# Batch 0 of an FFT and mixture-of-experts kernel: its first stage handed to the second by twelve transfers inside SBUF

## The chip, the cores and the metric

The kernel runs on one core of a Trainium2 chip. The metric is the device time of one execution in microseconds (us). Before the change the median of 8 runs is 1258.31 us, the lowest 1257.81, the highest 1259.43.

## The reference

The input `x` has shape (8, 2496, 256): 8 batches of 2496 tokens with 256 channels, float32. The reference does two things in a row:

```
X = fft(fft(x, axis=1), axis=2).real        # over the sequence, then over the channels
t = X.reshape(19968, 256)
logits = t @ w_gate                          # 8 experts
e = argmax(logits); gate = softmax(logits)[e]
out = gate * (relu(t @ w1[e]) @ w2[e])       # w1[e]: 256 x 1024, w2[e]: 1024 x 256
```

Each token goes to one expert alone, so the kernel sorts the transformed tokens by expert and multiplies them in blocks.

## The kernel before

**Stages.** The transform over 2496 = 104 x 24 positions is done in two stages of matrix products. The *first stage* of a batch (`first`, lines 325 to 347) takes `x` in three thirds, one tile `xq` each ([112, 8, 256], 896 KB). VectorE (DVE) adds each row to its mirror and folds the channels (`fold`, `fold_d`); TensorE (PE) multiplies with the waves `con["w1"]`, two steps to a half (`half1`), twelve steps in all; ScalarE (ACT) copies a half from PSUM to `t1`, and when a third is whole, a transfer writes it to the DRAM tensor `Td[b]` (448 KB; on ACT's queue for batches 0 and 1, on SyncE's (SP) queue later). `first` is a generator of twelve steps. `regroup` (line 351) reads `Td[b]` back in another order into two tiles `t4`, which have the 120 rows of five groups on the partitions; a batch has NG = 11 such groups.

The *second stage* (`second`, line 361) turns the column H of `t4` (`pr`), multiplies each group with `m2` into `zz`, and multiplies stretches of 128 of `zz` with `rd` (`p3`), which gives half the channels and the router's logits at once; two DVE operations build the rows of 128 tokens and their mirrors (line 410), ACT writes the mirrored channels. After five stretches `route` (line 416) finds expert and place of 1280 rows, in three steps and a last part, and puts ten transfers into `waiting`. Such a transfer (`send`, line 462) is an indirect scatter of 128 rows on GpSimd's (POOL) queue into `Xs`, where the tokens stand by expert. A batch takes 20 of them. The second stage is a generator of 19 steps.

The *experts* (`experts`, line 730) take blocks of `Xs`: rows and weights are fetched on SP, rows transposed by DVE (`turn`), multiplied (`ph`, `py`), scaled by ACT and scattered to the output by POOL.

**Order.** The order is written out by hand: each engine and each queue runs its instructions in the order in which the program issues them. For batch 0 everything before the experts is at the end of the program: the loads of `x`, waves and tables; `first(0)` whole; the loads of batch 1; the two `regroup` of batch 0; then the products of `rt` with the router's weights (`pg`); then seven steps of batch 1's `first` (`early`); then `second(0)`, in which every other step is followed by one more step of `early`, and each step by one `send`. `early` ends with the two `regroup` of batch 1.

Then the main loop asks `experts` for work. Each `yield 0, False` of it runs one step of the side list and one `send`. The side list weaves the plan of the first blocks (`close(0)`) with batch 1's second stage and batch 2's first stage (`mixed(1)`). Once the plan's table is there, all rows of batch 0 are sent, the first blocks are fetched, nine more `yield 0, False` follow (line 784), and then comes the first turn, the transpose of the first block, and the first `ph`. Of the eighteen side steps up to there the last nine hold the rest of the plan and batch 1's second stage up to its fourth stretch.

**Counters.** The framework gives a transfer issued from SP or ACT one of eight completion counters in turn; the issuing engine waits where the counter's last transfer is still under way.

Of the kernel before, what the change touches and what calls it, by code (L numbers as in the profile page):

```python
# [12 lines left out]
F32 = mybir.dt.float32  # L13
BF16 = mybir.dt.bfloat16
I32 = mybir.dt.int32
ALU = mybir.AluOpType
# [16 lines left out]
HALF = -(-NG // 2)  # L33
LAST = NW * 128 - (NG - 1) * GP
NT = B * S
E, F = 8, 1024
FC = F // 128
# [9 lines left out]
def free(ap, offset, *dims):  # L47
    return bass.AP(ap.tensor, ap.offset + offset, [list(ap.ap[0])] + [list(d) for d in dims])
# [167 lines left out]
def kernel(ctx: ExitStack, tc, x, w_gate, w1, w2, out):  # L216
    nc = tc.nc
    vec, act, pool = nc.vector, nc.scalar, nc.gpsimd

    def mm(o, lhsT, rhs, start=True, stop=True, **kw):  # L220
        nc.tensor.matmul(o, lhsT=lhsT, rhs=rhs, start=start, stop=stop, **kw)  # L221
# [4 lines left out]
    def const_dram(name, v):  # L226
        return nc.inline_tensor(v, name=f"c_{name}").ap()
# [36 lines left out]
    consts = shape_consts()  # L264
# [4 lines left out]
    con, k = {}, 0  # L269
# [12 lines left out]
    waves = const_dram("w1", consts["w1"])  # L282

    def load(b, q):

        if b < B:
            xq = xp.tile([NP, 8, D], F32, tag="xq", name="xq", bufs=3)
            row = (b * NQ + q) * NA
            nc.sync.dma_start(out=xq[:].rearrange("p j d -> p (j d)"), in_=x[row:row + NP])
            ahead[b, q] = xq[0:NA]  # L290

    def fold_d(o, a, n):
# [29 lines left out]

    ahead = {}

    def first(b):
# [23 lines left out]
    base = con["cap"]  # L349

    def regroup(b, h):
        t4 = sp.tile([128, HALF, D], F32, tag="t4", name="t4")
        n = min(HALF, NG - h * HALF)
        nc.sync.dma_start(
            out=t4[:, 0:n], in_=bass.AP(Td[b].tensor, Td[b].offset + h * HALF * GP * D,
                                        [[D, 128], [GP * D, n], [1, D]]))
        ahead[b, "t4", h] = t4

    zz = cp.tile([128, 2, NW * 128], F32, name="zz")

    def second(b):
# [368 lines left out]
    def experts(todo):  # L730
# [44 lines left out]
        for k, (b, size, last, at) in enumerate(todo):  # L775
            n, m = size // 128, BIG // size
            if not k:
                while todo[0][:3] not in tabs:
                    yield 0, False
                fetch_some(0, 1)  # L780
                while b not in whole:
                    yield 0, True
                fetch_some(0)
                for _ in range(9):
                    yield 0, False
                for xT in turn(b, size, xbs[0][0]):
                    pass
# [20 lines left out]
            if both:  # L808
# [4 lines left out]
                parts = [slice(lo, lo + fp) for lo in range(0, FC // 2, fp)]  # L813
# [133 lines left out]
        yield from through(b)  # L947

    vec.memset(ones[:], 1.0)
    act.dma_start(out=con["w1"][:, 0:4], in_=waves[:, 0:4])  # L950
    load(0, 0)
    load(0, 1)
    nc.sync.dma_start(out=con["w1"][:, 4:], in_=waves[:, 4:])
    load(0, 2)
    nc.sync.dma_start(out=table[:], in_=const_dram("table", packed))
    nc.sync.dma_start(out=con["rt"][:], in_=const_dram("rt", consts["rt"]))
    nc.sync.dma_start(out=wg[:], in_=w_gate)
# [6 lines left out]

    tabs, whole = {}, set()
    todo = in_order()
    for _ in first(0):
        pass
    load(1, 0)
    load(1, 1)  # L970
    regroup(0, 0)
    regroup(0, 1)
    load(1, 2)
    nc.sync.dma_start(out=bt[:], in_=const_dram("blocks", cv))
    sent(unordered(nc.sync.dma_start(
        out=Xs[E * CAP:].rearrange("(k p) w -> p k w", k=BLK // 128), in_=bc(pad[:], 1, BLK // 128)), "xs"), 0)
# [104 lines left out]
```

## Time and profile before

| | us |
|---|---|
| median of 8 runs | 1258.31 |
| the profiled execution: its time | 1257.62 |
| the profiled execution: its span, first to last instruction | 1255.8 |
| PE busy | 1207.7 (96%) |
| DVE busy | 759.6 (60%) |
| POOL busy | 447.5 (36%) |
| ACT busy | 431.3 (34%) |
| batch 0: last third of x landed, first use by DVE | 17.74 |
| batch 0: third write to Td issued, on ACT | 25.75 |
| batch 0: two reads into t4 issued, on SP | 28.88 and 29.33 |
| batch 0: first product of the second stage (pr) | 33.75 |
| batch 0: first scatter on POOL | 53.13 |
| batch 1: reads into t4 issued; first product of its second stage | 55.02; 60.37 |
| batch 0: fetch of the first block issued | 82.84 |
| first turn: transpose on DVE, first expert product on PE | 86.56, 87.33 |

All times are from one profiled execution, counted from its first instruction. The profile has a busy time per engine, the same in 40 slices of the span, the clock that PE was granted, the queues of the DMA engines (q1 is SP's, q10 is ACT's, q0 is POOL's), a timeline, the waits with what ended them, and the chain of waits that ends with the last instruction. L221 is the line of the helper that issues every matmul, so PE's instructions are told apart by their tiles: `s` is the first stage, `pr`, `p` and `rk` are the second stage and routing, `ph` and `py` the experts.

### The profile page before, as it was taken

To read this page: it belongs to the slowest core of one execution; us is meant where nothing else is said; L and a number is where in the kernel's file an instruction comes from. 1 tells how busy PE (TensorE), PEld (TensorE's weight loads), DVE (VectorE), ACT (ScalarE), POOL (GpSimd) and SP (SyncE) were. 2 spreads that over 40 slices of the span, in tenths; PEclk is the share of its full clock that TensorE was granted. 3 is DMA by queue.
4 is the path that set the end of the run, shared out by engine and by line. 5 is a ranking of instruction groups with operands and counts; after the bars stand their busy time and mean duration, and the time that the engine had idled before them with its cause. 6 is when DMAs were issued, how large, how long until landed. Compare 5 with 4: busy or idle time off the path is not lost.

```text
span 1255.8 us, 22295 instructions
## 1 busy us (share of the span) xinstructions
PE 1207.7 (96%) x7289; PEld 1076.2 (86%) x7289; DVE 759.6 (60%) x1804; ACT 431.3 (34%) x1167; POOL 447.5 (36%) x527
## 2 busy tenths in 40 slices
PE   5749999999999999999999999999999999999997
PEld 4648988777788899888988899889999999999996
DVE  4446434343456688566865578686888784444653
ACT  1424333333243433434343333432333332222222
POOL 0245427054117421471226613472364241111112
PEclk6869999999999999999999999999999999999999
DMA  8859898873548434673336435453346328888887
GB/s 242 280 177 337 305 313 310 222 242 117 151 154 263 147 117 156 189 232 113 102 128 208 137 98 166 135 177 101 107 138 187 113 106 285 276 286 284 280 290 284
DMA packets 163216, 249.79 MB, mean 199 GB/s; under 512 B 118601, under 2 KB 130227, under 8 KB 143516
## 3 DMA queue, kind: packets, MB, share of 16 engines
q1 hardware_dynamic: 146327, 203.28, 50.8%
q0 software_dynamic: 15888, 42.14, 9.1%
q10 hardware_dynamic: 885, 2.94, 0.7%
q8 instruction: 59, 0.97, 0.3%
q14 instruction: 57, 0.47, 0.1%
HBM read 194.91 MB, written 54.83 MB: 199 GB/s over the span
## 4 chain that ended last, share of the span: by engine, by line
PE 82%; DVE 9%; DMA 3%; ACT 2%; issue 2%; POOL 0%; SPq 0%; POOLq 0%; DVEq 0%; ACTq 0%
PE py L221 25%; PE ph L221 13%; PE a L221 11%; PE c L221 9%; PE p L221 6%; PE b L221 6%; PE d L221 5%; PE e L221 4%; PE s L221 3%; DMA xq<-in_x_dram 1%; DVE xT L584 1%; DMA Td<-t 1%; DVE y L684 1%; DMA Xs<-rows,pi 1%; DVE hT L636 1%
## 5 line engine op out<-in xcount | busy, mean ns | idle before, releaser
L236 POOL DMA_INDIRECT out_dram<-y,ro x163 | 161.5, 991 | 625.2 <-ACT y L680 301.2
L221 PE MATMUL py<-w_sb,hT 128*128 128x256 f32 x1504 | 339.5, 379 | 0.0
L221 PEld LDWEIGHTS py<-w_sb,hT 128*128 128x128 f32 x1504 | 281.4, 190 | 36.9 <-issue 1.0
L236 POOL DMA_INDIRECT Xs<-rows,pi x160 | 162.5, 1016 | 109.9 <-DVE rows L410 54.6
L221 PE MATMUL ph<-xT,w_sb 128*128 128x128 f32 (+2 forms) x992 | 171.6, 329 | 11.1 <-DVE xT L584 11.0
L221 PEld LDWEIGHTS ph<-xT,w_sb 128*128 128x128 f32 x992 | 136.7, 193 | 35.1 <-issue 16.8
L410 DVE SCALAR_TENSOR_TENSOR rows<-p,zs 128x129 f32<-128x129 f32 x160 | 48.9, 348 | 129.8 <-ACT lg L408 125.8
L221 PE MATMUL a<-xT,w_sb 128*128 128x256 f32 (+1 forms) x512 | 117.8, 357 | 0.0
L838 DVE TENSOR_SCALAR hT<-ph 128x512 f32<-128x512 f32 x43 | 29.7, 691 | 123.7 <-PE ph L221 64.0
L587 ACT ACTIVATE xT<-xT 128x256 f32<-128x256 f32 (+1 forms) x94 | 36.5, 388 | 179.0 <-DVE xT L584 140.6
L892 ACT ACTIVATE y<-py,xb 128x256 f32<-128x256 f32 x94 | 44.6, 475 | 152.3 <-PE py L221 152.1
L221 PEld LDWEIGHTS a<-xT,w_sb 128*128 128x128 f32 x512 | 88.6, 190 | 9.7
L636 DVE TENSOR_TENSOR hT<-hT,b 128x512 f32<-128x512 f32 x57 | 39.2, 687 | 75.8 <-PE b L221 50.2
L646 ACT ACTIVATE hT<-a 128x512 f32<-128x512 f32 x57 | 34.0, 597 | 134.1 <-PE a L221 131.1
L221 PE MATMUL s<-xq,w 104*112 104x256 f32 (+2 forms) x208 | 61.4, 418 | 15.2 <-DVE xq L297 11.1
L469 POOL CAST pi<-due 128x1 int32<-128x1 f32 x140 | 44.9, 320 | 66.7 <-ACT due L468 66.6
L221 PE MATMUL a<-w_sb,hT 128*128 128x128 f32 x528 | 66.0, 276 | 0.0
L221 PEld LDWEIGHTS a<-w_sb,hT 128*128 128x128 f32 x528 | 63.1, 192 | 0.7
L221 PEld LDWEIGHTS p<-table,t 120*128 120x128 f32 x352 | 53.4, 201 | 11.0 <-ACT t L372 2.8
L221 PE MATMUL c<-xT,ws 128*128 128x256 f32 (+1 forms) x256 | 60.3, 362 | 1.0 <-DVE hT L642 0.2
L584 DVE STREAM_TRANSPOSE xT<-xb 128x512 f32<-128x512 f32 (+1 forms) x91 | 56.2, 631 | 7.5 <-DMA xb<-Xs 7.5
L221 PE MATMUL p<-table,t 120*128 120x120 f32 (+1 forms) x352 | 56.6, 285 | 3.0 <-ACT t L372 2.0
(149 smaller groups left out, 2054.5 us busy)
## 6 DMA issues: line engine op xcount, KB each, us to landing
w_sb<-in_moe_w_dram SPq DMA_DIRECT2D x132, 1024.0 KB, 6.8
xq<-in_x_dram SPq DMA_DIRECT2D x24, 896.0 KB, 8.7
xb<-Xs SPq DMA_DIRECT2D x112, 128.0 KB, 3.4
Td<-t SPq DMA_DIRECT2D x18, 448.0 KB, 5.4
t<-Td SPq DMA_DIRECT2D x8, 768.0 KB, 6.9
t<-Td SPq DMA_DIRECT2D x8, 640.0 KB
xb<-Xs SPq DMA_DIRECT2D x52, 64.0 KB, 4.4
xb<-Xs SPq DMA_DIRECT2D x88, 32.0 KB, 4.4
```

Source lines behind the costliest of these rows:

```text
L221: nc.tensor.matmul(o, lhsT=lhsT, rhs=rhs, start=start, stop=stop, **kw)
L236: return unordered(pool.indirect_dma_start(out=dst, out_offset=bass.IndirectOffsetOnAxis(ap=idx, axis=0), in_=rows, in_offset=None, bounds ...
L410: vec.scalar_tensor_tensor(rows[:, k + m, 0:NY], p3[:, 0:NY], zs[:, 0:1], zs[:, 1:], op0=ALU.add, op1=op)
L469: pool.tensor_copy(idx, due[:])
L584: vec.transpose(free(xT[:], 256 * h, [32, n // 32], [BIG, 2], [1, 32]), free(xb, 512 * h, [64, n // 32], [1, 2], [2, 32]))
L587: act.activation(odd, odd, ACTF.Copy, scale=-1.0)
L636: vec.tensor_tensor(h12, h11, b[:], op=add)
L646: act.activation(h11, a[:], ACTF.Relu)
L684: vec.tensor_tensor(o, o, p[:], op=add)
L838: vec.tensor_scalar(o, ph[:], 0.0, None, op0=ALU.max)
L892: act.activation(y[:, i % 2], py[:], ACTF.Copy, scale=meta[:, i, 1:2])
```

## The change

In batch 0 the first stage no longer goes through `Td[0]`. The waves are loaded in another order of columns (`wp`, 110 columns of NG by ten), so that the product of step s has on its partitions, for each of ten (group row, part) pairs, the eleven groups. A new function `first_whole` does batch 0's first stage: it adds, folds and multiplies by halves of a third; after each half ACT copies it to `t1` (the last half in two copies), and each step is sent by a transfer of its own from `t1` to every twelfth partition of `t4s`, 110 KB in rows of 1 KB. Eleven of the twelve go on ACT's queue, that of step 11 on SP's. `t4s` is one tile for both halves of all groups; the `regroup` of later batches writes into it. Three ACT copies (`natural`) bring the waves back to the old order in `con["w1"]` for the later batches, whose unused columns DVE sets to zero.

The last third of `x` is loaded in two pieces, and the waves in three, with the pieces in between. `load(1, q)` is issued right after third q of batch 0. Three steps of batch 1's `first` stand before `second(0)` instead of seven, and twelve `yield 0, False` before the first turn instead of nine.

```
+    wp = bp.tile([128, NS + 3, NR], F32, tag="w2", name="wp", bufs=3)[0:NA]
+    order = consts["w1"][:, :, 0:NR].reshape(NA, NS + 3, NG, 2 * NU).swapaxes(2, 3)
+    waves = const_dram("w1", order.reshape(NA, NS + 3, NR))
...
+    def first_whole():
+        pm0 = xp.tile([NA, D], F32, tag="pm0", name="pm0")
+        for q in range(NQ):
+            xq = ahead.pop((0, q))
+            t1 = xp.tile([NP, 4, D], F32, tag="t1", name="t1")
+            for lo in (0, 2):
+                end = q == NQ - 1 and lo
+                a, m = xq[:, lo:lo + 2], xq[:, 4 + lo:6 + lo]
+                n = 2
+                if end:
+                    n = 1
+                    fold_d(pm0[:], m[:, 1], 1)
+                vec.tensor_tensor(a[:, 0:n], a[:, 0:n], m[:, 0:n], op=ALU.add)
+                fold_d(m, a, 2)
+                ps = pm_.tile([NP, 2, D], F32, tag="m", name="s1")
+                for i in range(2):
+                    s = 4 * q + lo + i
...
+                        mm(o, columns(s), m[:, i])
...
+                if end:
+                    for i in range(2):
+                        act.copy(t1[0:NR, lo + i], ps[0:NR, i])
+                else:
+                    act.copy(t1[0:NR, lo:lo + 2], ps[0:NR])
+                for i in range(2):
+                    s = 4 * q + lo + i
+                    (nc.sync if s == NS - 1 else act).dma_start(out=t4s[s:GP:NS, 0:NG], in_=t1[0:NR, lo + i])
+            load(1, q)
+        for lo in range(0, NS + 3, 5):
+            natural(lo, lo + 5)
+        for h in range(2):
+            ahead[0, "t4", h] = t4s[:, h * HALF:(h + 1) * HALF]
...
+    def natural(lo, hi):
+        n = hi - lo
+        act.copy(free(con["w1"][:, lo:hi], 0, [NP, n], [2 * NU, NG], [1, 2 * NU]),
+                 free(wp[:, lo:hi], 0, [NR, n], [1, NG], [NG, 2 * NU]))
...
     def regroup(b, h):
-        t4 = sp.tile([128, HALF, D], F32, tag="t4", name="t4")
+        t4 = t4s[:, h * HALF:(h + 1) * HALF]
...
+    t4s = cp.tile([128, 2 * HALF, D], F32, name="t4s")
...
-                for _ in range(9):
+                for _ in range(12):
                     yield 0, False
...
-    act.dma_start(out=con["w1"][:, 0:4], in_=waves[:, 0:4])
+    vec.memset(con["w1"][:, :, NR:], 0.0)
+    act.dma_start(out=wp[:, 0:4], in_=waves[:, 0:4])
     load(0, 0)
     load(0, 1)
-    nc.sync.dma_start(out=con["w1"][:, 4:], in_=waves[:, 4:])
-    load(0, 2)
+    nc.sync.dma_start(out=wp[:, 4:8], in_=waves[:, 4:8])
+    rest = load(0, 2, 2)
+    next(rest)
+    nc.sync.dma_start(out=wp[:, 8:], in_=waves[:, 8:])
+    next(rest)
...
-    for _ in first(0):
-        pass
-    load(1, 0)
-    load(1, 1)
-    regroup(0, 0)
-    regroup(0, 1)
-    load(1, 2)
+    first_whole()
...
     early = ahead_of(1)
-    for _ in range(7):
+    for _ in range(3):
         next(early)
```

More of the change, by code (lines that the diff above doesn't have):

```diff
@@ L34 @@
 LAST = NW * 128 - (NG - 1) * GP
+NR = 2 * NU * NG
 NT = B * S
@@ L281, with load @@
     ones = cp.tile([128, 128], BF16, name="ones16")
-    waves = const_dram("w1", consts["w1"])
-    def load(b, q):
+    wp = bp.tile([128, NS + 3, NR], F32, tag="w2", name="wp", bufs=3)[0:NA]
+    order = consts["w1"][:, :, 0:NR].reshape(NA, NS + 3, NG, 2 * NU).swapaxes(2, 3)
+    waves = const_dram("w1", order.reshape(NA, NS + 3, NR))
+    def load(b, q, parts=1):
         if b < B:
@@ L288, in load, with pieces @@
             row = (b * NQ + q) * NA
-            nc.sync.dma_start(out=xq[:].rearrange("p j d -> p (j d)"), in_=x[row:row + NP])
             ahead[b, q] = xq[0:NA]
+            if parts == 1:
+                nc.sync.dma_start(out=xq[:].rearrange("p j d -> p (j d)"), in_=x[row:row + NP])
+                return iter(())
+            return pieces(xq, row)
+    def pieces(xq, row):
+            for k in range(2):
+                nc.sync.dma_start(
+                    out=xq[:].rearrange("p (c j) d -> p c j d", c=2)[:, :, 2 * k:2 * k + 2],
+                    in_=x[row:row + NP].rearrange("p (c j d) -> p c j d", c=2, d=D)[:, :, 2 * k:2 * k + 2])
+                yield
     def fold_d(o, a, n):
@@ L323, with columns @@
     ahead = {}
+    def first_whole():
[15 more added lines that the diff above has]
+                    s = 4 * q + lo + i
+                    o = ps[0:NR, i]
+                    if s < NS - 1:
+                        mm(o, columns(s), m[:, i])
+                        continue
+                    for k, l, r in ((NS - 1, 0, H + 1), (NS + 1, H + 1, D)):
+                        mm(o[:, l:r], columns(k), pm0[:, l:r], True, False)
+                        mm(o[:, l:r], columns(k + 1), m[:, 1, l:r], False, True)
+                if end:
[11 more added lines that the diff above has]
+            ahead[0, "t4", h] = t4s[:, h * HALF:(h + 1) * HALF]
+    def columns(s):
+        return wp[:, s]
+    def natural(lo, hi):
+        n = hi - lo
+        act.copy(free(con["w1"][:, lo:hi], 0, [NP, n], [2 * NU, NG], [1, 2 * NU]),
+                 free(wp[:, lo:hi], 0, [NR, n], [1, NG], [NG, 2 * NU]))
     def first(b):
```

## The prediction

> **What bounds the kernel now.** Read first: the page's totals and slices, to see which engine is the bound and where it is not.
>
> ```profile
> span 1255.8 us, 22295 instructions
> PE 1207.7 (96%) x7289; PEld 1076.2 (86%) x7289; DVE 759.6 (60%) x1804; ACT 431.3 (34%) x1167; POOL 447.5 (36%) x527
> ...
> PE   5749999999999999999999999999999999999997
> PEclk6869999999999999999999999999999999999999
> ```
>
> PE is full from the fourth slice on; only the first three have holes, and a lower clock. Next, busy time by window over the start (columns PE, PEld, DVE, ACT, POOL, granted clock, DMA share, GB/s):
>
> ```profile
> 33.75:52.18 18.43, 15.77 (x97) 13.61 (x97) 8.63 (x34) 9.01 (x32) 0.00 (x0) 0.86 0.93 272
> 52.18:61.90 9.72, 5.78 (x44) 5.09 (x44) 5.93 (x29) 4.43 (x18) 6.94 (x7) 0.86 0.77 265
> 61.90:76.40 14.50, 9.29 (x47) 7.46 (x45) 12.20 (x56) 4.83 (x17) 11.45 (x11) 0.74 0.68 240
> 76.40:87.33 10.93, 0.00 (x1) 0.00 (x1) 2.71 (x8) 0.67 (x4) 3.89 (x4) 0.65 0.33 95
> 87.33:94.00 6.67, 6.67 (x21) 5.79 (x22) 0.29 (x2) 2.00 (x6) 0.00 (x0) 0.54 0.65 195
> 94.00:1255.80 1161.80, 1150.16 (x7024) 1030.99 (x7022) 715.76 (x1649) 404.32 (x1081) 425.04 (x503) 1.00 0.60 196
> ```
>
> After 94 us PE is idle for 11.6 us of 1162. So the end moves with the first turn (87.33, the first expert matmul), and by PE work done before it that would otherwise follow it. All else counts only as it moves these two. What sets the first turn is in the timeline and the chain of waits:
>
> ```profile
> 14.46 0.59 ACT t L321
> 15.07 9.50 DMA Td<-t
> ...
> 25.13 0.60 ACT t L321
> 25.75 3.06 DMA Td<-t
> ...
> 63.54 3.60 DMA Xs<-rows,pi
> ...
> 80.23 2.37 DMA Xs<-rows,pi
> ...
> 84.45 1.99 DMA xb<-Xs
> 86.56 0.72 DVE xT L584
> 87.33 3.78 PE ph L221 x8
> ```
>
> The chain runs: first stage of batch 0, its write to Td (landed 28.8), the read back (pr, the first matmul on it, at 33.75), second stage and routing of its first half (idx ready 52.18), then 20 scatters on POOL from 53.13 to 81.2 (1.28 us each when nothing disturbs, 28.1 in all), the fetch of the first block, the transpose. One more view, queues over 15 to 19.9 us, while two Td writes had been issued on ACT:
>
> ```profile
> q1 hardware_dynamic: 482, 1.23, 101.4%
> ```
>
> and over 20 to 26 us:
>
> ```profile
> q1 hardware_dynamic: 181, 1.32, 57.6%
> q10 hardware_dynamic: 219, 0.82, 38.9%
> ```
>
> ACT's queue (q10) got not one packet while SP's (q1) worked off x, the table and rt. Td 0, issued at 15.07, landed at 24.57, and the third t1 copy stood 5.7 us for its buffer.
>
> **The change part by part.** Sums are differences in the profiled execution, whose own time is 1257.62 (span 1255.8 and 1.8 around it), 0.7 below the median of the runs, 1258.31; I take the difference from the median.
>
> *First stage by halves.* The last third of x still lands near 17.7: the bytes ahead of it are the same. After it DVE did 2.86 us (17.74 to 20.6); now only the second half waits for it: pm0 0.48, an add of 256 elements about 0.33 (between 0.29 for 127 and 0.69 for 508), a fold of half size about 0.8, together 1.6, so 19.3. PE had 3.56 us (20.68 to 24.24); the other half is done before, 2.7 remain: 22.0. Copies go singly, about 0.35 each, so the last step is issued near 22.5, where before the third write was issued at 25.75.
>
> *Twelve DMAs for three writes and two reads.* Removed: the write's landing (3.06) and the read (28.88 to 33.75). Added: eleven issues on ACT of 0.31 = 3.4 us against 0.9, between copies, beside PE. The twelfth goes on SP, and behind it stand load(1,2), bt, the pad rows and load(2,·); SP also loses two reads and their wait. A step is 110 packets of 1 KB. No row shows SBUF to SBUF; the nearest are 1 KB packets from DRAM (1046 in 3 us on 16 engines, 46 ns each on one) and the Td write on an idle queue, 3.06 for 448 KB. Lower bound: about 2.5 from issue to landing, t4s complete at 25. Upper bound: held as Td 0 was, 4.9 us before the first packet, complete at 30. Steps issued from 12 us on stand beside the same q1 load, but the last four come when most of it is through: I take 27.5, the middle, against 33.75. Behind a step held on ACT stand the copies of the next half, and PE behind those (three PSUM buffers).
>
> Here the Trainium skill speaks on both sides. DMA: Bandwidth & Descriptors, section "Queues, rings and completion order", has each engine alternate between queues; the row above, 482 packets against none, does not show that at 15 us. By the rule alone t4s would stand at 25 and the sum below would be 1250.0; by the row, 30 and 1255.0. The section on why a DMA adds 16 to its semaphore says a copy runs on the largest number of engines up to 16 that divides both sides' partition counts: 110 and 10 give 10, not 16. That agrees with the 104-partition load of w on q10, 117 packets, 104 and 13 completions. By it a step takes 11 packets per engine instead of 7, about 0.2 us longer, less than 1 us over the last four.
>
> *Waves transposed back.* Three ACT copies of 550 elements, about 0.63 each (512 take 0.59): 1.9 us, from about 22.7 to 24.6, under the landing of the last steps. Without that cover they would hold ACT's first copy of the second stage by as much. The memset on DVE and two more load issues on SP (0.44 each) lie in the wait for the first x.
>
> *Three steps ahead instead of seven.* Second stage up to idx took 18.43. Out of it go: DVE's wait for load(1,2) (first rows could start at 40.8, started at 41.73) and one half of products before the first rows (about 1.1 to 1.6 at the low clock): minus 2. Into it come, on DVE, pm0 and add of the third x (1.45) and its fold (1.5), both in front of rows or routing: plus 2.95. So 19.4: idx at 46.9, 5.3 earlier. If only POOL counted (35.15 from idx to turn), the turn would come at 82.0.
>
> *What is late next.* Batch 1's own write now comes after product halves that sit in the second half of batch 0's second stage. Its last half comes after the products of h1's last rows (55.1 to 56.4 before; now about 52.8 and 0.9 more), copy and write as before behind load(2,2) (48.68 to 55.02 was 6.3): regroup(1) at about 60 against 55.02, pr of batch 1 at 65 against 60.37. From pr its rows need 7.5 (half clock): 72.4, before 72.14. From there to the end of DVE's list 6.9 as before (72.14 to 79.07), and the three further steps: rows 0.6, routing part one 1.5, a fold 1.35, part two 0.4, with ACT and PE between about 3.6 in all. Then the transpose 0.75: turn at 83.7. This is later than POOL's 82.0, so it sets it: 3.6 earlier than 87.33. Before, DVE had 7.5 us of slack here; now none.
>
> *Twelve steps ahead of the turn instead of nine.* Products of the fifth rows (two groups of 4, 0.60 and 0.67 at full clock) and one half of batch 2's products (0.88) go from behind the turn into idle PE: 2.2. The sends are unaffected: none waits at that point.
>
> *Clock.* 6.67 us at 0.54 after the turn lost 3.1. The hole ahead of the turn gets shorter, so some may come back; or nothing. I count 0 and keep 3 for the range.
>
> Sum: -3.6 - 2.2 = -5.8, 1252.5.
>
> **Rivals.**
> - *The steps stand behind SP's queue* as Td 0 did, and the third quarter's copies behind them for a t1 buffer: t4s at 30 to 33, turn 86.2 to 89.2, with the moved work 1255.0 to 1258.0. For it: each Td write met this (15.07, 33.64, 39.92 all started some 4 to 5 us late). Against: at 25.75, with q1 nearly empty, none.
> - *Slower: the steps go one after another.* If a step waits on ACT until the one before has landed (the framework taking interleaved partitions of t4s for overlapping, or too few completion counters; wg stood 2.6 us for w's), twelve times 0.31 and some 2 us (the shortest landing in the trace, 1.8) from 12 us give t4s at 40, 12.5 later than I take it: 1265. It decides from t4s at 33.3 (no gain), slower by 0.2% from 35.8. Against it: Td 1 was issued at 18.96 with Td 0 still in flight into column strips of the same rows.
> - *Hidden anyway.* Batch 1's chain with three more steps puts the turn at 87.3 whatever t4s does; only the moved products remain: 1256.1. For it: DVE is 84% busy from 61.9 to 76.4. Against: its list ended 7.5 before the turn.
>
> **How the numbers follow.** Forecast 0.60, behind the queue 0.18, one after another 0.14, hidden 0.08. Forecast with t4s 25 to 30 and 0 to 3 of clock: 1247 to 1255. What a measurement here can tell from no change is about 0.2%, 2.5 us. Faster by more: nearly all of the first, under half of the second and fourth: 0.69. Slower: nearly all of the third, a little of the others: 0.16. Same: 0.15. The range takes in the second and fourth and the mild end of the third: 1246 to 1262.
>
> **What would show it.** Right: t<-Td gone for batch 0, pr at 25 to 30, first scatter near 48, first ph near 84 with DVE or xb just ahead of it, s x4 and p between 78 and 84, PE after that as full as before. The queue rival: no q10 packets until 20 us and a t1 copy released by a t4s DMA. The serial rival: ACT issues 2 us apart, each ended by the landing of the last. Wrong if PE has new holes after the turn, if batch 1's t4 comes later than 65, or if DVE's list ends after 87.

## The result

The change makes the kernel slower. Over 12 runs its median is 1263.8 us (1262.95 to 1266.2); the kernel before has 1259.09 beside it (34 runs). The ratio is 1.0040, 95% interval 1.0032 to 1.0047. The profiled execution has a span of 1260.4 us against 1255.8, 4.6 longer. The same kernel before takes some 1259 us on some chips and some 1274 on others, so each ratio below is against runs of it on the same chip.

Busy time by window over the start of the changed kernel. The boundaries are the issue of the load of batch 1's second third, batch 0's first product of the second stage, its index ready, the index of its second half, batch 1's first `pr`, the first turn, and 100 us. The columns are PE, PEld, DVE, ACT, POOL, granted clock, DMA share, GB/s.

```profile
20.30:34.04 13.74, 2.04 (x8) 1.89 (x9) 5.54 (x12) 4.19 (x7) 0.00 (x0) 0.53 0.74 193
34.04:52.22 18.18, 15.13 (x84) 12.85 (x84) 8.37 (x33) 9.07 (x30) 0.00 (x0) 0.78 0.46 136
52.22:63.81 11.59, 8.83 (x58) 7.81 (x57) 6.03 (x29) 6.00 (x22) 8.13 (x9) 0.87 0.76 213
63.81:75.16 11.35, 0.00 (x0) 0.03 (x1) 9.84 (x43) 0.00 (x0) 9.00 (x8) 0.58 0.86 273
75.16:92.37 17.21, 11.69 (x64) 9.96 (x64) 8.57 (x36) 7.82 (x29) 3.89 (x4) 0.80 0.65 224
92.37:100.00 7.63, 7.63 (x39) 6.32 (x39) 1.24 (x5) 1.86 (x4) 0.00 (x0) 0.74 0.87 289
100.00:1260.40 1160.40, 1147.20 (x6994) 1028.80 (x6992) 711.50 (x1631) 401.92 (x1077) 424.82 (x503) 1.00 0.59 195
```

Batch 0's second stage stands where it stood: `pr` at 34.04 (33.75), index at 52.22 (52.18). Batch 1's first `pr` stands at 75.16 (60.37), and ahead of it PE has not one matmul in 11.35 us. The first turn comes at 92.37, 5.0 later than 87.33. Behind it PE works 7.63 + 1147.20 = 1154.8 us (1156.8 before, 2.0 less) and is idle for 13.2 (11.6). The account is 5.0 - 2.0 + 1.6 = 4.6, the difference of the spans.

The chain of waits (start, duration, what; only the pieces that speak) has a new middle. The first block ends in batch 0's first reading, the second in the first turn:

```profile
10.92 0.59 ACT t L368
...
11.53 8.68 DMA t4s<-t
...
20.30 9.29 DMA xq<-in_x_dram
...
29.61 0.79 ACTq L371
...
30.44 0.65 ACT t L366 x2
...
31.11 2.79 DMA t4s<-t
...
34.04 0.54 PE pr L222 x2
```

```profile
61.42 7.27 DMA Td<-t
...
68.75 6.28 DMA t4s<-Td
...
75.16 0.54 PE pr L222 x2
...
90.12 0.68 DVE xq L309
90.80 0.60 DVE xq L310
...
91.48 0.14 DVE lg L497
...
91.71 0.61 DVE xT L646
```

Steps are counted from 0. Step 0 is issued at 11.53 and landed at 20.2. The loop's load of batch 1's second third, whose completion counter is that of step 0, is issued only then; it lands at 29.59, and step 9, whose counter is that of this load, is issued at 29.61. The last step follows at 31.11 and the reading at 34.04. From 86.28 on DVE's list runs without a gap up to the transpose: it ends last there, through batch 1.

The fetch of the rows is late as well, though not last. The last scatter is issued at 79.09 (80.23 before), but lands only at 84.99, 5.9 us later (2.37 before), beside other transfers on SP's queue, and the fetch follows it. SP's issues of that fetch, in the changed kernel and, below, in the kernel before:

```profile
85.24 1.92 SPq L598 DMA_DIRECT2D xb<-Xs  x4
```

```profile
82.84 1.92 SPq L536 DMA_DIRECT2D xb<-Xs  x4
```

Before, the first product followed 4.5 us after this fetch. By that distance the fetch alone would put the turn at 89.7, so that, as an estimate, 2.4 of the 5.0 us would be there without DVE's list.

PE had the products of the last step done at 19.55, and ACT copied them at 30.44; in the 11 us between stand ACT's earlier copies and issues, and their waits:

```profile
19.17 0.38 PE L222 MATMUL s<-xq,wp 104*110 104x127 f32 x2
```

ACT over 10 to 38 us shows the same from the side of the engine (in brackets the idle time before, and what ended it):

```profile
16.98 0.58 ACT L368 COPY t<-s 110x512 f32<-110x512 f32 x1 [3.08 <-DMA xq<-in_x_dram]
17.91 6.79 ACTq L371 DMA_DIRECT2D t4s<-t  x2
24.74 0.59 ACT L368 COPY t<-s 110x512 f32<-110x512 f32 x1 [7.18 <-DMA t4s<-t]
...
30.84 0.79 ACTq L371 DMA_DIRECT2D t4s<-t  x1
31.67 3.26 ACT L383 COPY w<-wp 104x550 f32<-104x550 f32 x3 [0.58 <-ACT t L366]
```

The two issues of steps 4 and 5 take 6.79 us, because step 5 waits for its counter, that of step 1, which lands at 23.89. An issue that waits for nothing takes 0.79 us; the writes to `Td` took 0.31. The three strided copies of the waves, which batch 1's products read, come last, from 31.67 on.

### The profile page after: what moved, and what is told of

Its sections match the earlier page's. It is cut to its first block, busy times and chain, and to the rows that moved or that the text cites. A ratio compares the mean times of both kernels' runs of the same rounds, so it can differ in the third digit from the quotient of the medians.

```text
span 1260.4 us, 22323 instructions
## 1 busy us (share of the span) xinstructions
PE 1204.7 (96%) x7289; PEld 1075.7 (85%) x7289; DVE 760.8 (60%) x1817; ACT 434.1 (34%) x1171; POOL 446.0 (35%) x527
## 4 chain that ended last, share of the span: by engine, by line
PE 67%; issue 16%; DVE 8%; DMA 3%; POOL 3%; ACT 2%; POOLq 0%; ACTq 0%; DVEq 0%; SPq 0%
PE py L222 20%; PE a L222 9%; PE ph L222 8%; PE c L222 8%; PE p L222 6%; PE b L222 5%; PE d L222 4%; PE s L222 3%; PE e L222 3%; POOL out_dram L237 3%; DMA xq<-in_x_dram 1%; DVE xT L646 1%; DMA t4s<-t 1%; DVE y L746 1%; DMA Td<-t 1%
## 5 line engine op out<-in xcount | busy, mean ns | idle before, releaser
L222 PEld LDWEIGHTS p<-table,t4s 120*128 120x128 f32 x352 | 54.0, 203 | 9.9 <-ACT t4s L434 3.2
L222 PE MATMUL p<-table,t4s 120*128 120x120 f32 (+1 forms) x352 | 56.8, 286 | 2.5 <-ACT t4s L434 2.5
L222 PE MATMUL b<-xs,ws 128*128 128x256 f32 (+1 forms) x256 | 58.7, 357 | 0.0
L222 PE MATMUL c<-xs,ws 128*128 128x256 f32 (+1 forms) x256 | 58.7, 356 | 0.0
```

## The experiments

**How to compare them.** They ran in six groups, each on one chip (A on chip 0, B and E on 6, C and D on 3, F on 1) beside its own runs of the kernel before, and every ratio is against those. The ratio on record is not the quotient of the two medians; for `late_nine` that quotient is 1.0022, so steps of 0.2% say little. In the traces of groups A, B and E engines stand for 3 to 14 us on no named work, at varying places; single times of these traces count little.

| run | group | median us | before, same group | ratio, 95% interval |
|---|---|---|---|---|
| nine_steps | A | 1276.76 | 1273.63 | 1.0025 (1.0007 to 1.0042) |
| before_twelve | A | 1274.4 | 1273.63 | 1.0004 (0.9976 to 1.0031) |
| early7 | A | 1282.24 | 1273.63 | 1.0051 (1.003 to 1.0071) |
| handover_only | A | 1288.43 | 1273.63 | 1.0107 (1.0075 to 1.014) |
| before_three_early | B | 1277.24 | 1274.48 | 1.0021 (1.0008 to 1.0035) |
| split_seven | B | 1273.3 | 1274.48 | 0.9986 (0.9971 to 1.0001) |
| loads_after | B | 1278.14 | 1274.48 | 1.0025 (1.0007 to 1.0044) |
| loads_after_split | B | 1281.34 | 1274.48 | 1.0061 (1.0041 to 1.0081) |
| change_again | C | 1263.62 | 1258.69 | 1.0038 (1.0023 to 1.0052) |
| split_seven_again | C | 1261.01 | 1258.69 | 1.0020 (1.0006 to 1.0035) |
| split_nine | C | 1259.81 | 1258.69 | 1.0008 (0.9996 to 1.002) |
| loads_late_steps_late | C | 1282.97 | 1258.69 | 1.0198 (1.0177 to 1.0219) |
| copies_split | D | 1258.96 | 1259.23 | 1.0003 (0.9993 to 1.0013) |
| copies_split_nine | D | 1259.6 | 1259.23 | 0.9998 (0.9988 to 1.0008) |
| dense_nine | D | 1261.37 | 1259.23 | 1.0019 (1.001 to 1.0029) |
| late_six | E | 1280.18 | 1273.64 | 1.0063 (1.0039 to 1.0087) |
| late_nine | E | 1276.49 | 1273.64 | 1.0041 (1.002 to 1.0062) |
| plan_first | F | 1273.03 | 1259.91 | 1.0107 (1.0087 to 1.0126) |

The theory after the result: the hand-over gains nothing because its transfers stand behind other traffic and other counters, and the time is lost in batch 1, whose first stage comes later. The first rival: the twelve steps ahead of the turn are the loss.

### The smaller parts, one at a time

The counts of steps, in the change and in the kernel before.

```
 nine_steps (the change)               before_twelve (the kernel before)
-                for _ in range(12):   -                for _ in range(9):
+                for _ in range(9):    +                for _ in range(12):
```

> The changed kernel with nine steps before the turn as before; three early steps stay. Theory (batch 1's chain is late at its first product, 75.16, whatever follows): that product stays near 75, DVE's list ends after the third x's pm0 and add near 88, the turn comes near 89.5, and the 2 us of products go behind it again: 1262 to 1264, no better than the change. Rival (the three further steps are the loss): 1258.5 to 1260.

> The kernel before with twelve steps before the turn instead of nine, nothing else. Theory: DVE's list had 7.5 us of slack before the transpose, the three steps take about 4 of it, the turn stays at 87.3, and about 2 us of products go from behind it into idle PE: 1256.5 to 1257.5 against 1259. Rival (the three steps delay the turn): 1260 or more.

The change with nine steps stays 1.0025 slower, and the kernel before with twelve is 1.0004, with an interval that ends at 1.0031 and so leaves out a loss of the change's size. The twelve steps are not the whole loss; whether they are part of it (1.0025 here, 1.0040 for the change, in different groups) is not shown.

```
 early7                                handover_only
-    for _ in range(3):                 as early7, and
+    for _ in range(7):                -                for _ in range(12):
                                       +                for _ in range(9):
```

> The changed kernel with seven steps of batch 1's first stage before batch 0's second instead of three; twelve steps before the turn stay. Theory (the loss is batch 1's chain, which the three early steps make late; the hand-over itself neither gains nor loses, since pr stood at 34.04 against 33.75): batch 1's reads into t4 are issued near 56 instead of 68.75, its pr is near 61 instead of 75.16, the first turn near 87.5 and set by the fetch of the first block again, and the products moved ahead of it bring about 2 us: 1256 to 1258 with before at 1259. Rival (the three further steps before the turn are what makes it late): the turn stays at 90 or later, 1261 to 1263.

> The changed kernel with seven early steps and nine steps before the turn, so that only the twelve transfers, the halves and the order of loads are left of the change. Theory: batch 0's pr near 34, the turn near 87.5, 1258 to 1260, the time of before. Rival (the twelve transfers cost time themselves, by the ACT queue or by the DMA engines): 1261 or more.

These two say less than they were meant to. `t4s` is one tile for both halves (groups 0 to 5 and 6 to 10) of every batch. With seven early steps the program writes batch 1's rows into its second half ahead of batch 0's groups 6 to 10, so these two kernels compute batch 0's second half from batch 1's rows, and PE waits for that transfer. What follows is that three is not a free choice: with two plain `regroup` at the end of `early`, batch 1 may not reach them before batch 0 has read its last group. The next run gets round this.

```
 before_three_early (the kernel before)
-    for _ in range(7):
+    for _ in range(3):
```

> The kernel before with one digit changed: three of batch 1's first steps ahead of batch 0's second stage instead of seven; nothing of the hand-over, of the loads or of the nine steps is touched, and it has a read tile for each half. Theory: batch 1's last write to DRAM goes from 49.7 to about 58 to 62, its pr from 60.4 to about 68 to 75; DVE's folds for it stand behind batch 0's routing; the first turn comes 1 to 5 us later than 87.3; time 1.001 to 1.004 of before. Rivals (the hand-over itself, its DMAs, or the twelve steps are the loss): the turn stays within 0.5 us of before, time 0.9995 to 1.0005.

The early count alone, in a kernel without any hand-over, takes 1.0021 of before in group B. The amount is as the theory had it, but it was run in this group alone, and a ratio of group B below differs from its repetition in C by 0.0034, so the amount is not safe. Its trace is one of those with a hole (SP stands for 14 us from 52), so how much later batch 1 comes is not read from it.

### Seven early steps in the change

```
-    early = ahead_of(1)
-    for _ in range(3):
+    early = first(1)
+    for _ in range(7):
         next(early)
     for k, _ in enumerate(second(0)):
         if k % 2 == 0:
             next(early, None)
+        if k in (10, 14):
+            regroup(1, (k - 10) // 4)
         send()
```

> The change, with seven of batch 1's first steps ahead of batch 0's second stage again (as in the kernel before) instead of three; each half of the one read tile is asked for by batch 1 as soon as batch 0's last group of that half is written down, so both batches still have their own rows. Theory (batch 1's first stage is late because only three steps are early, and the hand-over gains nothing): first reading of the hand-over about 34 us as in the change, the hand-over's index 52 to 54, batch 1's pr 60 to 66 instead of 75.2, the transposes no longer behind it on DVE, first turn at about 87 to 88.5 instead of 92.4; the time 4 to 5 us under the change's, 0.997 to 1.000 of before. Rival (twelve steps between the fetch and the turn are the loss): the early steps give nothing, turn at 91 or later, time 1.003 to 1.005 of before. Rival (seven early steps on PE, ACT and DVE hold up batch 0's second stage, whose rows come at the same moment as before): index 55 or later, POOL's scatters end 2 us or more later, time 1.001 to 1.003.

> The change itself, unedited, beside the three versions it is to be compared with on one chip. Theory and rivals alike: about what it was beside the kernel before the first time, 1.002 to 1.005 of before; batch 1's pr at 75 to 82, first turn 5 us or more behind that of the kernel before. If it comes at 1.000 here, the loss is a matter of the chip and no experiment on it tells anything.

> The change with seven early steps and batch 1's reads asked for by halves, for a second time, beside the unedited change. Theory (three early steps instead of seven are the loss): 3 to 6 us under the change on the same chip, 0.997 to 1.000 of before. Rival (the early steps are only part of it): 1 to 2 us under the change, 1.001 to 1.003 of before.

In group C, beside the unedited change, the split is 1.0020 against 1.0038, about half of the loss, and in group B 0.9986. The intervals in C overlap, and B's is not the one of C (in B and its like the holes fall at other places in each kernel), so the traces of C have to say the rest. Batch 1's `pr` goes from 75.09 to 66.72, but the first turn only from 92.84 to 91.52, because batch 0's own `pr` goes from 33.29 to 37.94, and with it the index (56.05) and the last scatter (83.34). That was the third case of the expectation. PE and ACT over 20 to 40 us show what holds it:

```profile
28.29 1.02 PE L222 MATMUL pg<-wg,rt 128*128 128x8 f32 x4 [0.33 <-DVE table L1047]
34.40 3.75 PE L222 MATMUL s<-xq,w 104*112 104x256 f32 x8 [5.09 <-ACT w L383]
37.94 0.42 PE L222 MATMUL pr<-t4s,table 120*120 120x6 f32 x2
```

```profile
32.35 0.79 ACTq L371 DMA_DIRECT2D t4s<-t  x1
33.18 3.28 ACT L383 COPY w<-wp 104x550 f32<-104x550 f32 x3 [0.58 <-ACT t L366]
```

PE stands 5.09 us for a strided copy of the waves, for batch 1's first products, which stand ahead of batch 0's `pr` in PE's order. The copies stand behind the last transfer that ACT issues. In the prediction they were hidden under the landing of the last steps; that cover holds only while no product of batch 1 is early.

Nine steps in place of twelve:

> The same with nine steps between the fetch and the first turn, as in the kernel before: what is left of the change is the hand-over from SBUF to SBUF alone, with its folds and products by halves. Theory (the hand-over gains nothing, since its first reading comes at 34 as before, and loses nothing): within 0.0015 of before either way, first turn within 1 us of the version with twelve. Rival (the transfers, their waits on ACT's queue or the three strided copies cost by themselves): 1.002 or more of before. Rival (twelve steps are worth their 2 us of products): 1 to 2 us slower than the version with twelve.

1.0008 against 1.0020, with intervals that overlap: no difference is shown, and a gain from twelve is not seen.

### The copies moved

On top of the seven early steps, the three copies of the waves go behind the transfer of step 4.

```
                     (nc.sync if s == NS - 1 else act).dma_start(...)
+                    if s == 4:
+                        for n in range(0, NS + 3, 5):
+                            natural(n, n + 5)
...
-        for lo in range(0, NS + 3, 5):
-            natural(lo, lo + 5)
```

> The change with seven early steps (reads by halves) and the three strided copies of the waves (which batch 1's products read) put on ACT right behind the transfer of step 4, where ACT stands 5 us for step 1's landing, instead of behind the last transfer. With the split alone batch 1's first product began 3 us after the last transfer was issued, because the copies stood behind it, and batch 0's pr behind that product at 37.9. Theory (the copies behind ACT's held queue are the rest of the loss): first product of batch 1 at 30 to 32 instead of 34.4, first reading 34 to 35, index 52 to 53.5, POOL's scatters end 79 to 80.5, batch 1's pr 61 to 64, first turn 87 to 89; time 0.997 to 1.000 of before. Rival (PE's order, with the seven steps' products, holds the first reading whatever the copies do): first reading 36.5 or later, turn 90 or later, 1.001 or more.

> The same with nine steps between the fetch and the turn. Theory: first turn 86 to 88, about 1.5 us earlier than with twelve, and 1 to 2 us more of products left for later, 0.997 to 1.0005 of before; with the split alone nine was 1.2 us the faster at the median. Rival (PE's order holds the first reading): 1.0005 or more, as nine with the split alone (1.0008).

Both come level with the kernel before: 1.0003 and 0.9998. ACT does the copies where it stood for step 5's counter, and PE's first early products wait for DVE's fold alone (PE and ACT of the version with twelve steps, 20 to 40 us):

```profile
31.39 3.75 PE L222 MATMUL s<-xq,w 104*112 104x256 f32 x8 [2.92 <-DVE xq L311]
34.94 0.42 PE L222 MATMUL pr<-t4s,table 120*120 120x6 f32 x2
```

```profile
19.74 3.24 ACT L384 COPY w<-wp 104x550 f32<-104x550 f32 x3 [1.32 <-DMA table<-c_table]
24.62 0.79 ACTq L371 DMA_DIRECT2D t4s<-t  x1
```

The end of its chain ahead of the turn is that of the kernel before, to a few tenths of a microsecond (80.23, 84.45, 86.56, 87.33 there):

```profile
80.17 2.69 DMA Xs<-rows,pi
...
84.71 2.03 DMA xb<-Xs
86.76 0.71 DVE xT L647
...
87.53 3.78 PE ph L222 x8
```

So the loss is undone by these two edits together: 1.0003 (up to 1.0013) against 1.0038 (from 1.0023) for the change itself, both on chip 3. The copies moved alone, with three early steps, were not run, and the intervals of neighbours overlap; the shares of the two edits (1.0038, 1.0020, 1.0003) are not shown singly. What remains of the change, the hand-over itself with its twelve transfers, gains nothing that the interval shows: `pr` at 34.94, index at 52.06, turn at 87.53.

### Is there a gain in the hand-over?

First the loads of batch 1, which in the change go between the thirds, were put behind all of batch 0's first stage.

```
-            load(1, q)
+        for q in range(NQ):
+            load(1, q)
```

> The change, with batch 1's three loads put behind the whole of batch 0's first stage on SP instead of one behind each third, so that none of them stands ahead of, or beside, the twelve transfers, and none shares a completion counter with them before they are asked for. Theory (the transfers wait for SP's traffic and counters, not for themselves): step 0 lands 2 to 4 us after it is issued instead of 8.7, the first reading of the hand-over at 25 to 29 instead of 34.0, the index at 44 to 48; batch 1's first stage starts later by its loads (its first product at about 36 to 40 instead of 33) but the three early steps hold less ahead of it; first turn 86 to 91; time 0.997 to 1.001 of before. Rival (the twelve transfers are slow by themselves, ten packet groups each): first reading 32 or later, the rest as in the change or later, time 1.003 to 1.006. Rival (batch 1's loads then come late themselves): first reading early, but batch 1's pr at 76 or later and the turn at 92 or later, time 1.003 to 1.006.

> Both edits together: batch 1's loads behind batch 0's first stage, and seven steps early with its reads asked for by halves. Theory, if both edits do what is said of them alone: first reading 25 to 29, index 46 to 50, batch 1's pr at 56 to 62, first turn 82 to 85, time 0.994 to 0.998 of before, which beats both kernels. Rival (the seven steps stand on the engines until batch 1's loads have come, and hold batch 0's second stage): index 52 or later in spite of the early reading, time 0.998 to 1.002. Rival (twelve transfers slow by themselves): as the version with the split alone.

The last step is issued at 27.50 instead of 31.11 and the first reading comes at 30.57: without batch 1's loads between the steps, their bytes and their counters, it is 3.5 us earlier, not the 5 to 9 of the theory. Two things are left above the 27.5 predicted. Step 3 waits until 19.1 for step 0, which stands behind SP's first loads. And from there on ACT waits for no landing, yet needs 8.4 us to the last step: two issues of 0.79 and a copy of 0.58 make some 2.3 us for every two steps. But the gain is gone at once: batch 1's first third now lands at 35.8 us, and its products stand in the middle of batch 0's second stage. PE of that kernel:

```profile
30.57 0.54 PE L222 MATMUL pr<-t4s,table 120*120 120x6 f32 x2 [5.08 <-DMA bt<-c_blocks]
30.96 2.09 PE L222 MATMUL p<-table,t4s 120*128 120x120 f32 x8
38.49 2.05 PE L222 MATMUL s<-xq,w 104*112 104x256 f32 x4 [5.45 <-DVE xq L311]
```

With seven early steps it is worse: PE waits 12.9 us for the same load ahead of `pr`, which comes at 42.46.

Then batch 1's steps were moved behind their loads.

```
-    for _ in range(3):
-        next(early)
     for k, _ in enumerate(second(0)):
-        if k % 2 == 0:
+        if k > 3 and k % 2 == 0:
```

> Batch 1's three loads behind batch 0's first stage on SP, and none of batch 1's first steps ahead of batch 0's second stage: they begin with its fifth step, when the first load has landed, and the rest comes between the fetch and the turn. In the version with the loads moved alone batch 0's first reading came 3.5 us earlier and PE then stood 5.5 us on batch 1's first third; here nothing of batch 1 stands ahead of it. Theory (the hand-over's gain is there and is eaten by whatever of batch 1 stands in the engines' order before its load): first reading 29 to 31, index 46 to 49, POOL's scatters end 73 to 78; the twelve steps then hold most of batch 1's first stage; first turn 82 to 90, time 0.996 to 1.002 of before. Rival (the second stage is slower beside the loads, or the twelve steps with batch 1's folds hold DVE until after the rows are there): index 51 or later, or first turn at 92 or later, time 1.003 or more.

Here the hand-over's gain is seen: `pr` at 30.79, index at 47.54 (4.6 earlier), the last scatter at 74.91 (5.3 earlier). Yet the version is 2% slower (1.0198). Its chain, and below it the waits over 60 to 112 us (engine and line, releaser, total, times, longest):

```profile
74.91 6.57 DMA Xs<-rows,pi
...
89.73 8.69 DMA t4s<-Td
```

```profile
PE pr L222 <- DMA t4s<-Td: 34.0, 1, 34.0
```

Batch 1's read stands on SP behind the fetch of the first turn's rows and is issued at 89.73; its `pr` stands ahead of the turn on PE, which waits for 34 us. Three runs, all with batch 1's loads behind batch 0's first stage, try to take this away. `dense_nine` has batch 1's steps at every step of the second stage from the fifth on (`if k > 3:`), nine steps and the copies moved; `late_six` and `late_nine` keep every other step and emit the rest of batch 1's first stage, with its reads, ahead of the fetch:

```
     for k, _ in enumerate(second(0)):
         ...
+    for _ in early:
+        send()
     work = experts(todo)
...
-                for _ in range(12):
+                for _ in range(6):        # late_nine: 9
```

> Batch 1's loads behind batch 0's first stage, none of batch 1's steps ahead of the second stage, one at every step of it from the fifth on (instead of every other), so that batch 1's reads are asked for before the fetch of the first turn's rows, the copies behind step 4, and nine steps before the turn. The version with the loads and the steps late had batch 0's index at 47.5 and POOL's end at 74.9, 5 us earlier than any other, and lost 34 us of PE to batch 1's pr, whose read stood on SP behind that fetch. Theory (the hand-over's gain is real and reaches the turn once nothing of batch 1 stands in its way): first reading 30 to 31, index 47 to 50, POOL's scatters end 75 to 78, batch 1's pr 66 to 74, first turn 82 to 87, time 0.995 to 1.000 of before. Rival (one step of batch 1 at every step of batch 0 slows the second stage by what the earlier reading gave): index 51.5 or later, POOL's end 79 or later, turn 87 or later, 1.000 to 1.004.

> The version with batch 1's loads and steps late, with two edits: what is left of batch 1's first stage is emitted right behind batch 0's second stage, so that its reads stand on SP ahead of the fetch of the first turn's rows; and six steps instead of twelve stand between that fetch and the turn, so few that batch 1's pr comes behind the turn on PE. Theory (the hand-over gives 4 to 5 us to batch 0's index, and all of it was lost to batch 1's pr ahead of the turn): first reading 30 to 31, index 47 to 49, POOL's scatters end 74 to 77, first turn 80 to 85 with PE not waiting for batch 1, time 0.993 to 0.999 of before, the first version to beat the kernel before. Rival (what batch 1 does later comes back behind the turn, as PE idle time): turn 80 to 85, but idle time of PE after it 16 us or more instead of 11.7, time 0.999 to 1.003. Rival (products of batch 1's first stage behind the second stage hold PE beyond the fetch): turn 86 or later, 1.000 or more.

> The same with nine steps, as in the kernel before: batch 1's pr is then the last but one of what stands ahead of the turn. Theory: its read lands at 72 to 79 and holds PE until then and little longer, first turn 82 to 88, some 1 to 4 us behind the version with six; time 0.996 to 1.001 of before. Rival (the second stage and not batch 1's order sets the turn): within 0.5 us of the version with six.

`dense_nine` (1.0019) is its rival: first reading 33.31, index 52.18. The copies behind step 4 cost in this order, where ACT had less idle time (step 6 is issued at 25.50, in the version without them at 23.02), and the second stage took 18.87 us instead of 16.75 with the interleaved steps. In `late_six` (1.0063) and `late_nine` (1.0041) the index is early (48.10 and 47.20), the last scatter too (76.95 and 75.89), and batch 1's `pr` still comes ahead of the turn, at 82.15 and 80.70, with PE standing 16.6 us for it. I had overlooked that the steps that run while the plan is made already hold it; six or nine made no difference to that. In `late_six`, however, this is not what sets the turn (92.28): the last scatter lands 7.40 us after its issue, and the fetch behind it takes 5.28. The last run, on top of `late_six`, puts the plan ahead of batch 1's second stage:

```
-            side = woven(chain(close(0), through(0)), chain(early, side))
+            side = chain(close(0), through(0), side)
```

> The version with six steps, with one further edit: the planning of batch 0's blocks is no longer woven with batch 1's second stage but goes whole ahead of it, so that nothing that reads batch 1's rows stands ahead of the first turn on PE, ACT or DVE. In the version with six steps batch 1's pr still came ahead of the turn (82.15 against 92.28), with DVE standing 15 us for its rows ahead of the transposes. Theory (the hand-over's 4 to 5 us are in batch 0's index and scatters, and only batch 1 stands between them and the turn): index 47 to 49, POOL's end 75 to 77, first turn 80 to 85; idle time of PE behind it grows, as batch 1's rows come later; time 0.994 to 1.001 of before. Rival (what batch 1 does later is lost again): turn as early, and time 1.002 or more, with batch 1's index at 110 or later. Rival (the fetch itself is late for another reason): turn 88 or later.

Now nothing of batch 1 stands ahead of the turn (its `pr` is at 95.82), the index is at 48.69, the last scatter at 76.85, and the turn still comes at 92.24. The chain, and the queues over 77 to 84.5 us (packets, MB, share of 16 engines):

```profile
76.85 7.41 DMA Xs<-rows,pi
84.26 0.02 SPq L599
...
86.11 5.34 DMA xb<-Xs
```

```profile
DMA packets 1593, 2.12 MB, mean 283 GB/s; under 512 B 75, under 2 KB 1483, under 8 KB 1537
## 3 DMA queue, kind: packets, MB, share of 16 engines
q1 hardware_dynamic: 1496, 1.90, 81.6%
q0 software_dynamic: 97, 0.22, 9.0%
```

The last scatter takes 7.41 us to land (2.37 before), beside batch 1's read, some 1400 packets of 1 KB that now pass at this moment, and the fetch behind it 5.34 (1.99 before), beside two weight loads that SP issued at 78.64 and 79.21. This is the "other reason" of the expectation's last rival. That these bytes are what slows both is argued from their time alone; no run moved them. The turn is the smaller part of the loss: of the 15.4 us by which the span is longer, 4.9 are the turn, 8.4 are PE work that now follows it (1165.2 us against 1156.8), as batch 1 is 19 us late (first index at 119.38 against 100.41), and 2.1 are idle time. No version run here beats the kernel before by more than its interval.

## Why the prediction was wrong, by its own steps

- **Twelve DMAs: "I take 27.5, the middle, against 33.75."** This step failed. The steps were complete at 33.90. The lower and upper bounds (25 and 30) counted the wait for SP's packets once, for the last steps alone. What happened is a row of three waits: step 0 without a packet behind SP (four steps stood issued, and q10 had none between 12 and 17 us), step 5 for the counter of step 1 until 23.9, and step 9 for the counter of `load(1,1)` until 29.61. The rivals "behind SP's queue" (30 to 33) and "one after another" (40, through too few counters) each had a part of it; neither had the load of batch 1 between the steps, which the diff shows. Taking batch 1's loads away gave 3.5 us back.
- **In the same step: "eleven issues on ACT of 0.31 = 3.4 us."** Mis-sized: an issue of such a step took 0.79 to 0.91 us, eleven 8.8. The 0.31 was the price of a write to `Td`. With its copies ACT needs some 2.3 us for two steps, so that a wait in the middle is not made up. In `loads_after` seven issues stand behind the last wait and ahead of the last copies; at 0.31 they would take some 3.4 us less, as an estimate, which is more than the 2.7 by which its steps are complete after 27.5 (30.2).
- **First stage by halves: PE done at 22.0.** Right, and better: 19.55. The loss is all behind it, on ACT and in the queues.
- The rule weighed there, on queues taking turns (the Trainium skill, DMA: Bandwidth & Descriptors, "Queues, rings and completion order"), gave 25, the row 30. The trace of the change sides with the row at first; the queues of the changed kernel over 12 to 17 us (packets, MB, share of 16 engines) list SP's alone:

```profile
q1 hardware_dynamic: 534, 1.28, 105.2%
```

Over 17 to 24 us both queues move, q10 0.43 MB beside 1.18 of q1.

- **"regroup(1) at about 60 against 55.02, pr of batch 1 at 65 against 60.37."** The mechanism was right and the size was off: 68.75 and 75.16. As an estimate, some 6.5 of it is the first term's error, as batch 1's products stand behind batch 0's `pr` (first at 36.48); the rest is the landing of the last write, 7.27 us where it took 5.35 before, and the read.
- **DVE's list sets the turn.** Right: from batch 1's `pr` to the transpose I counted 17.9 us (65 to 82.9); 16.5 were measured. With its `pr` at 75.16 the prediction's own sum gives 93.9 for the turn, beside 92.37. What the prediction did not have is that the fetch comes late too (85.24 for 82.84), by the landing of the last scatter.
- **Second stage up to the index, 19.4.** It took 18.2, no slower than before.
- **Waves transposed back, 1.9 us under the landing of the last steps.** They took 3.26, and the cover was there in the change but for some 0.3 us (`pr` done at 34.58, ACT's copy of it at 34.83). With early products of batch 1 the cover is gone, and the runs show what they then cost: 3 us of batch 0's `pr`.
- **Twelve steps: 2.2 us moved ahead.** PE's work behind the turn did fall by 2.0, but the cause is not shown: between nine and twelve steps it differs by 0.3 (1155.4 and 1155.1, the split) and 0.6 (1156.6 and 1156.0, the copies moved). Part of the 2.0 is the clock, of which I counted none: 0.74 over the 7.6 us behind the turn, 0.60 over the same stretch before, which is some 1.0 us as an estimate (7.63 x 0.74 less 7.67 x 0.60).
- **PE after the turn as full as before.** Nearly: 13.2 us idle against 11.6.
- **The signs of being wrong that it named.** Two came: batch 1's reads into `t4s` later than 65 (68.75), and DVE's list ending after 87 (91.6).

Put into the prediction's sum of -5.8: 6.5 for the steps (34.0 for 27.5), 2.2 for what batch 1 is late beyond that (92.37 for 83.7, less 6.5), 1.6 for idle time behind the turn and 0.2 for the moved work give +4.7, beside 4.6 measured. The sum closes because its terms are the measured ones; that the turn would have come 6.5 earlier with the steps at 27.5 is the prediction's own rule, and no run here shows it. Where the hand-over did come earlier (30.79, index at 47.54), the turn did not.

## What to carry to other kernels

In this kernel every version that made batch 0's path shorter paid for it in batch 1's. Before giving a new path a time, list every transfer that the program puts between the new ones, and whose completion counter each of them takes, and look up what one issue costs the engine that issues them. An engine's early steps for the next batch are an order, not a gift: they help when their data are there, and hold everything behind them when they are not. A copy moved to the end of a queue costs nothing only as long as nobody reads its result early; ask who reads it, and what stands behind that reader.

## What was unexpected in the hardware's behaviour

- An indirect scatter's landing took 2.37 us with the queues nearly idle and 5.9, 6.57 and 7.41 beside other transfers; its issue on POOL took 0.97 us in the first case and 0.98 in the last and shows nothing of it.
- ACT needed 0.79 us to issue a transfer of 110 rows of 1 KB from SBUF to SBUF, where a write of 448 KB to DRAM took 0.31.
- ACT's three strided copies of 550 elements took 3.26 us, 1.09 each, where a copy of 512 elements out of PSUM takes 0.59.
- In the traces of groups A, B and E engines stand on no work that is named, SP for 14 us in one of them. The cause was not looked for.
